# One piece of an MLP product moved from the first attention steps back into the MLP, with the second key tile's scores put ahead of it

## The chip, the core and the metric

The kernel runs on one NeuronCore of a Trainium2 chip. Five engines work side by side, each with its own queue of instructions that it takes in order: TensorE (PE; its loads of weights are listed as PEld), VectorE (DVE), ScalarE (ACT), GpSimd (POOL) and SyncE (SP, which here only issues transfers). An instruction whose inputs are not ready stops its engine, and all that is queued behind it, until they are. Matrix products land in PSUM, which has eight banks of 128 x 512 float32 values. The metric is the device time of one execution in microseconds (us), lower is better.

## The reference

For x of shape 2048 x 448 (one sequence) two branches are computed and mixed token by token:

```python
g = _sigmoid((x * gate_w).sum(-1, keepdims=True))
# A: attention, 16 heads of 28, one shared key and value head
q = (x @ wq) as 16 heads;  k = x @ wk;  v = x @ wv
o = softmax(q k^T * 28 ** -0.5) v
a = o @ wo
# B: token mixing by shifted columns, then an MLP
h  = _gelu(_layernorm(x) @ w1)
x1 = x + shifted(h) @ w2
b  = x1 + _gelu(_layernorm(x1) @ w3) @ w4      # w3: 448 x 1792, w4: 1792 x 448
out = g * a + (1 - g) * b
```

The change touches the last 128 of the 1792 rows of w4, for the last 512 tokens only, and the first three of the sixteen key tiles of the first attention unit.

## The kernel before

The program has three stages, written in the order in which each engine is to run its instructions: the schedule is manual, so an engine's queue is the order of the Python statements.

**First stage (0 to about 125 us).** Queries, keys, values and the gate; the token mixing branch; x1. The queries are written to DRAM (`qd`) and read back later, 512 tokens of four heads at a time, by `q_load` (four transfers on SP's queue).

**MLP (about 125 to 399 us).** For each of four blocks b of 512 tokens, `w3_part(b, f)` makes one 128 x 512 piece f (0 to 13) of the hidden layer: eleven products in fp32r, one of the float32 formats, with each operand split into a high and a low part. ScalarE applies the gelu twice, to an fp32r tile `gh` and a float32 tile `gf`, and VectorE forms the low part `gl = gf - gh`. Two pieces later `w4_part(f, t, ...)` adds the piece's product with w4 into four PSUM accumulators `acc[t]`, one for 128 tokens each: three matmuls (`gh`·`w4h`, `gh`·`w4l`, `gl`·`w4h`) for each t, so twelve matmuls a piece. After the last piece VectorE adds `acc[t]` to `x1`. The weights come in seven pairs of pieces, each loaded by SP and split by `split_w3` and `split_w4` during block 0.

In the kernel before, piece 13 of block 3 is an exception. Its gelu is kept as one float32 tile `gf_late`, its part of w4 was loaded as a plain float32 tile `w4_late`, and its product is left for the attention stage: eight *jobs* (`w4_products` and `w4_add`), one for each 128 tokens and each half of the 448 columns. A job is four float32 matmuls side by side in the array (`by_columns`, line 844; the profile counts two instructions for each) and one VectorE instruction (line 879) that weighs the result by 1 - g and adds it to x1.

**Attention (about 396 us to the end).** There are 16 units u (four token blocks times four groups of four heads) and 16 key tiles of 128 keys in each. For one unit and key tile, `scores` makes four heads' scores, 128 keys x 512 queries each, in three rounds of four matmuls that run side by side in four row groups of the array (line 204). `exps` (line 257, ScalarE) turns them into the tile `p`. `values` (line 893) multiplies p by the values.

A *step* c of the main loop handles two key tiles, 2c and 2c + 1; there are 128 steps. The eight PSUM banks are four *singles* and two *pairs* of two adjacent banks. The even tile of a step has heads 0 and 1 in two singles and heads 2 and 3 in one pair; VectorE copies the pair to the tile p in SBUF (line 954) and ScalarE exponentiates it there later, which frees the pair early. The odd tile uses the other two singles and the other pair, which ScalarE reads directly. After the scores of a step stand the values of the step before (32 instructions, written into the singles that the exps have emptied), and after those at most one job. In ScalarE's queue a step is: two singles, two singles, one pair, and last the exp of the copied tile (`p<-p`). So one `p<-p` row marks one step.

Steps 0 and 1 fill this pipeline. Tile 0 is computed at the end of the MLP, between the w4 products of piece 11 and of piece 12. In step 0 of the kernel before come tile 1 (four singles), tile 2 (both pairs, which are the four accumulators' banks: `pair_0` lies over acc 0 and 3, `pair_1` over acc 1 and 2) and three jobs. Step 1 makes tile 3 and the values of tiles 0 and 1. Steps 3, 5, 7, 9 and 11 hold one job each (`IDLE`), and the jobs of `wo` begin in step 12, one a step.

**Queues around the change.** At the start of the attention stage SP issues one 896 KB transfer of `wof` (the weights wo, first used in step 12) and behind it the four transfers of `q_fetch(1)`, the queries of unit 1, into `qr`. The memory that `wof` gets is that of `gh` tiles of the MLP, so this transfer waits for the last matmul that reads the last of them. In VectorE's queue `q_begin(1)` stands at step 2: a cast of `qr` to the fp32r tile `qh_1` (line 193), ahead of the copy of step 2's pair. In TensorE's queue, in the middle of step 2's values, stand sixteen small matmuls (`max_part`, line 211) that read `qh_1` and write into that same pair.

Of the kernel before, what the change touches and what calls it, by code (L numbers as in the profile page):

```python
# [17 lines left out]
P = 128  # L18
S = 2048
D = 448  # L20
H = 16
DH = 28
F = 1792
C = D // 4
NB = S // 512
NT = S // P
NF = F // P
# [15 lines left out]
def gated_mix_kernel(  # L43
# [64 lines left out]

    def split_w_high(raw, wh, wl):
        nc.scalar.copy(wh[:, 0:3, :], raw[:, 0:3, :])  # L110
        nc.gpsimd.memset(f32(wh)[64:128, 3, :], 0.0)
        nc.scalar.copy(wh[0:64, 3, :], raw[0:64, 3, :])
        nc.scalar.copy(wl[64:128, 3, :], raw[64:128, 3, :])

# [4 lines left out]

    def split_w(raw, wh, wl):  # L120
        split_w_high(raw, wh, wl)
        split_w_low(raw, wh, wl)
# [133 lines left out]
    def exps(p, heads, source=None):  # L256
        nc.scalar.activation(p[:, heads], p[:, heads] if source is None else source, AF.Exp, scale=SCALE)  # L257
# [4 lines left out]
    with tc.tile_pool(name="s1b", bufs=1) as s1b, \  # L262
# [329 lines left out]
        ql0 = late.tile([P, 512], F32R, name="ql0")  # L592
        gf_late = late.tile([P, 512], F32, name="gf_late")
        w4_late = late.tile([P, D], F32, name="w4_late")
        bigs = ctx.enter_context(tc.tile_pool(name="bigs", bufs=1, side="right", reuse_waits="tile"))
# [5 lines left out]
        def big(name):  # L601
            return bigs.tile([P, 2048], F32, tag="big", bufs=2, name=name)
# [12 lines left out]
        def split_w3(i):  # L615
            split_w(raw3[i], w3h[i], w3l[i])

# [49 lines left out]
    with tc.tile_pool(name="s2", bufs=1, reuse_waits="tile") as s2, \  # L667
# [11 lines left out]
        def w3_part(b, f):  # L679
            i, k = divmod(f, 2)  # L680
            ps = mm_tile(f"g_{b}_{f}")
            proj(ps, w3h[i][:, :, k * P:(k + 1) * P], w3l[i][:, :, k * P:(k + 1) * P], *acts[b])
            if (b, f) == (NB - 1, NF - 1):
                nc.scalar.activation(gf_late, ps, AF.Gelu_apprx_tanh)
                return None
            gh = s2.tile([P, 512], F32R, tag="gh", bufs=3, name=f"gh_{b}_{f}")
            gl = s2.tile([P, 512], F32R, tag="gl", bufs=3, name=f"gl_{b}_{f}")
            gf = s2.tile([P, 512], F32, tag="gf", bufs=1, name=f"gf_{b}_{f}")
            nc.scalar.activation(gh, ps, AF.Gelu_apprx_tanh)  # L689
            nc.scalar.activation(gf, ps, AF.Gelu_apprx_tanh)  # L690
            nc.vector.tensor_sub(gl, gf, f32(gh))  # L691
            return gh, gl

        def w4_part(f, t, g, acc, stop=NF - 1):
# [4 lines left out]
            nc.tensor.matmul(ps, gh[:, tok], w4h[i][:, k, :], start=(f == 0), stop=False)  # L699
            nc.tensor.matmul(ps, gh[:, tok], w4l[i][:, k, :], start=False, stop=False)  # L700
            nc.tensor.matmul(ps, gl[:, tok], w4h[i][:, k, :], start=False, stop=(f == stop))  # L701

        for b in range(NB):
            acc = [ps2.tile([P, 512], F32, tag="acc", bufs=4, name=f"acc_{b}_{t}") for t in range(4)]
            gs = {}
            for f in range(NF):
# [43 lines left out]
            if b == NB - 1:  # L750
                singles = [mm_tile("bank_0"), mm_tile("bank_1"), misc_tile("bank_2"), max_tile("bank_3")]
                scores(0, 0, singles)
                nc.scalar.activation(first, powt, AF.Exp)
                p_first = big("p_0_0").rearrange("p (j n) -> p j n", j=4)
                for j in range(4):
                    exps(p_first, slice(j, j + 1), singles[j].unsqueeze(1))
            for t in range(4):
                w4_part(NF - 2, t, gs[NF - 2], acc, NF - 2 if b == NB - 1 else NF - 1)
                if b + 1 < NB:
                    ln_split(b + 1, t, t + 1)  # L760
            for t in range(4):
                if b < NB - 1:
                    w4_part(NF - 1, t, gs[NF - 1], acc)
                xt = x1[:, 4 * b + t, :]
                nc.vector.tensor_add(xt, xt, acc[t][:, 0:D])
# [4 lines left out]
    with tc.tile_pool(name="s3", bufs=1, reuse_waits="tile") as s3, \  # L770
# [70 lines left out]
        def by_columns(ps, a, t, w, start=True, stop=True):  # L841
            for i in range(4):
                c = t * P + 32 * i
                nc.tensor.matmul(ps[32 * i:32 * i + 32, :], a[:, c:c + 32], w, start=start, stop=stop,  # L844
                                 tile_position=(0, 32 * i))
# [27 lines left out]

        def w4_products(t, ps, cols):
            by_columns(ps, gf_late, t, w4_late[:, cols])

        def w4_add(t, ps, cols):
            n = NT - 4 + t
            nc.vector.scalar_tensor_tensor(x1[:, n, cols], ps, gi[:, n:n + 1], x1[:, n, cols],
                                           op0=ALU.mult, op1=ALU.add)  # L880

        p_of = {0: p_first}

# [13 lines left out]

        jobs = [(w4_products, w4_add, (t,), cols) for t in range(4) for cols in halves]
        left, right, both, front = slice(0, 1), slice(1, 2), slice(2, 4), slice(0, 2)
        sums, norms, later = [], [], []  # L900
# [16 lines left out]
        def run_jobs(ps, n):  # L917
            job_adds(job_products(ps, n))

        NC = NU * NT // 2  # L920
        JOBS_0 = (2, 1)
        IDLE = range(2, 12, 2)
        HINTS = {8 * NT // 2 + 4: [mybir.EngineType.SP],
                 14 * NT // 2 - 2: [mybir.EngineType.DVE, mybir.EngineType.Activation]}
        for c in range(NC):
# [3 lines left out]
            if c == 0:  # L929
                pb = score_tiles(u, 1, s2, s3_, s0, s1)  # L930
                for j, ps in enumerate((s2, s3_, s0, s1)):
                    exps(pb, slice(j, j + 1), ps.unsqueeze(1))
                pa = score_tiles(u, 2, *(q[:, h] for q in pairs for h in range(2)))
                nc.vector.tensor_copy(pa[:, front], pairs[0])
# [210 lines left out]
```

## Time and profile before

| | us |
|---|---|
| runs, three | 911.51, 911.80, 913.12 |
| median | 911.80 |
| profiled execution | 911.48 |
| its span (first to last instruction) | 909.70 |
| ScalarE busy in 500 to 600 us | 99.64 of 100 |
| TensorE busy in 500 to 600 us | 100.00 of 100 |
| loads of weights (PEld) busy in 500 to 600 us | 56.55 of 100 |

Times in the rows of the trace are counted from the start of the span. A row of the timeline gives the start, the busy time, engine, line, operation, output and input tile, shape and count of instructions; in square brackets stands how long the engine had been idle before it and what ended that. Matmuls are pipelined, so the busy times of neighbours overlap, and the distance between two starts is what one costs. The same holds for ScalarE: exps that follow each other start 0.48 us apart though each is listed with 0.6 us.

### The profile page before, as it was taken

How to read it: one execution, taken by the hardware profiler on the slowest of the kernel's cores; microseconds unless marked ns; L12 is line 12 of the kernel's file. 1: busy time of each engine (PE TensorE's matmuls, PEld its weight loads, DVE VectorE, ACT ScalarE, POOL GpSimd, SP SyncE). 2: the span in 40 equal slices, each digit the busy share in tenths (PEclk: the TensorE clock that was granted, in tenths of full speed). 3: DMA queues.
4: the chain of work that ended last, by engine and by line, in shares of the span. 5: the costliest groups of instructions: out<-in, count | busy, mean ns of one | idle time of the engine just before them, and what ended most of it. 6: DMA issues, size and time to landing. Idle time of an engine off the chain costs nothing.

```text
span 909.7 us, 24149 instructions
## 1 busy us (share of the span) xinstructions
PE 903.1 (99%) x10360; PEld 626.8 (69%) x10360; DVE 515.8 (57%) x960; ACT 632.6 (70%) x1003; POOL 79.1 (9%) x116
## 2 busy tenths in 40 slices
PE   9999999999999999999999999999999999999998
PEld 6788888888888888875555555555555555555554
DVE  3665273631441531136766777676767667767665
ACT  5542444332132231269999999999999999999995
POOL 3243320200000520020000000000000000000000
PEclk9999999999999999999999999999999999999999
DMA  8832653120110120010000001000011000010001
GB/s 294 289 103 61 147 167 129 37 70 1 39 49 2 22 65 1 1 52 24 14 25 14 24 15 56 23 25 17 25 33 36 24 14 25 15 55 14 15 14 44
DMA packets 40726, 47.31 MB, mean 52 GB/s; under 512 B 10152, under 2 KB 28904, under 8 KB 40616
## 3 DMA queue, kind: packets, MB, share of 16 engines
q1 hardware_dynamic: 37448, 40.43, 15.2%
q10 hardware_dynamic: 3168, 5.31, 1.6%
q8 instruction: 82, 1.34, 0.6%
q14 instruction: 28, 0.23, 0.1%
HBM read 32.56 MB, written 11.67 MB: 49 GB/s over the span
## 4 chain that ended last, share of the span: by engine, by line
PE 97%; ACT 2%; DMA 1%; DVE 0%; issue 0%; SPq 0%
PE bank L893 26%; PE bank L204 20%; PE bank L844 6%; PE acc L701 5%; PE acc L699 5%; PE acc L700 5%; PE g L135 4%; PE g L137 4%; PE g L136 4%; PE pair L204 2%; ACT p L257 2%; PE hs L475 1%; PE hs L476 1%; PE g L138 1%; PE g L139 1%; PE h L136 1%
## 5 line engine op out<-in xcount | busy, mean ns | idle before, releaser
L257 ACT ACTIVATE p<-bank 128x512 f32<-128x512 f32 x514 | 265.9, 605 | 4.4 <-POOL pick L866 1.5
L893 PE MATMUL bank<-p,vext 128*32 128x256 f32 x4064 | 247.7, 382 | 1.0 <-ACT p L257 1.0
L893 PEld LDWEIGHTS bank<-p,vext 128*32 128x32 f32 x4064 | 117.9, 110 | 115.9 <-ACT p L257 53.0
L954 DVE COPY p<-pair 128x1024 f32<-128x1024 f32 x125 | 153.0, 1224 | 57.9 <-PE pair L204 40.9
L689 ACT ACTIVATE gh<-g 128x512 fp32r<-128x512 f32 x55 | 32.9, 598 | 181.7 <-PE g L139 181.7
L818 DVE TENSOR_TENSOR o<-o,bank 128x256 f32<-128x256 f32 x222 | 93.5, 421 | 80.4 <-PE bank L893 72.3
L257 ACT ACTIVATE p<-p 128x1024 f32<-128x1024 f32 x126 | 138.0, 1096 | 0.0
L257 ACT ACTIVATE p<-pair 128x1024 f32<-128x1024 f32 x129 | 136.8, 1060 | 0.0
L691 DVE TENSOR_TENSOR gl<-gf,gh 128x512 fp32r<-128x512 f32 x55 | 38.6, 702 | 164.9 <-ACT gf L690 164.9
L204 PE MATMUL bank<-qh,kh 32*128 32x512 f32 x514 | 114.8, 443 | 0.0
L204 PE MATMUL pair<-qh,kh 32*128 32x512 f32 x510 | 114.0, 443 | 0.0
L204 PE MATMUL bank<-qh,kl 32*128 32x512 f32 x514 | 101.8, 389 | 0.0
L204 PE MATMUL bank<-ql,kh 32*128 32x512 f32 x514 | 101.6, 390 | 0.0
L204 PE MATMUL pair<-qh,kl 32*128 32x512 f32 x510 | 101.3, 389 | 0.0
L204 PE MATMUL pair<-ql,kh 32*128 32x512 f32 x510 | 100.9, 389 | 0.0
L204 PEld LDWEIGHTS bank<-qh,kh 32*128 32x128 f32 x514 | 48.0, 182 | 61.3 <-issue 38.7
L701 PE MATMUL acc<-w4h,gl 128*128 128x448 f32 x220 | 80.7, 367 | 0.0
L699 PE MATMUL acc<-w4h,gh 128*128 128x448 f32 x220 | 80.2, 364 | 0.0
L700 PE MATMUL acc<-w4l,gh 128*128 128x448 f32 x220 | 79.8, 363 | 0.0
L844 PE MATMUL bank<-wof,on 128*32 128x224 f32 (+1 forms) x984 | 69.6, 357 | 0.0
L135 PE MATMUL g<-ah,w3h 128*128 128x512 f32 x168 | 65.4, 389 | 0.0
L136 PE MATMUL g<-al,w3h 128*128 128x512 f32 x168 | 65.4, 389 | 0.0
(206 smaller groups left out, 1394.1 us busy)
## 6 DMA issues: line engine op xcount, KB each, us to landing
qd<-qf ACTq DMA_DIRECT2D x15, 256.0 KB
rb<-rd SPq DMA_DIRECT2D x15, 256.0 KB
x<-in_x_dram SPq DMA_DIRECT2D x4, 896.0 KB
xd<-xt SPq DMA_DIRECT2D x16, 224.0 KB
w34raw<-in_w_dram SPq DMA_DIRECT2D x7, 512.0 KB
qr<-qd SPq DMA_DIRECT2D x64, 56.0 KB
w34raw<-in_w_dram SPq DMA_DIRECT2D x7, 448.0 KB
out_dram<-ot SPq DMA_DIRECT2D x14, 224.0 KB
```

The source lines that it names most:

```text
L135: nc.tensor.matmul(ps, wh[:, c, :], ah[:, c, :], start=(c == 0), stop=False)
L136: nc.tensor.matmul(ps, wh[:, c, :], al[:, c, :], start=False, stop=False)
L204: nc.tensor.matmul(ps[j], k[h, keys], q[h, :], start=(r == 0), stop=(r == 2), tile_position=(32 * j, 0))
L257: nc.scalar.activation(p[:, heads], p[:, heads] if source is None else source, AF.Exp, scale=SCALE)
L691: nc.vector.tensor_sub(gl, gf, f32(gh))
L699: nc.tensor.matmul(ps, gh[:, tok], w4h[i][:, k, :], start=(f == 0), stop=False)
L700: nc.tensor.matmul(ps, gh[:, tok], w4l[i][:, k, :], start=False, stop=False)
L701: nc.tensor.matmul(ps, gl[:, tok], w4h[i][:, k, :], start=False, stop=(f == stop))
L818: nc.vector.tensor_add(o, o, pv)
L844: nc.tensor.matmul(ps[32 * i:32 * i + 32, :], a[:, c:c + 32], w, start=start, stop=stop, tile_position=(0, 32 * i))
L893: nc.tensor.matmul(pv[32 * j:32 * j + 32, :], vext[:, kt, :], p_of[k][:, j, qs], start=(k == ks[0]), stop=(k == ks[-1]), tile_position=(0, ...
L954: nc.vector.tensor_copy(pa[:, both], pairs[0])
```

## The change

Piece 13 of block 3 is treated like every other piece: its gelu gives `gh`, `gf` and `gl`, and `w4_part` adds its product into the accumulators, in the order of t 1, 2, 0, 3 (in all four blocks). `gf_late`, `w4_late`, its load, and the eight jobs are gone. The scores and exps of key tile 1 stand ahead of these twelve matmuls, in the four singles, and write a tile of another pool. Step 0 keeps only tile 2: two heads in the two singles that step 1 doesn't use, two in `pair_1`, which VectorE copies and ScalarE exponentiates from SBUF. A loop without jobs remains for steps 2 to 11, and `IDLE` goes. In `split_w3` the copy of the doubled last rows of w3 moves from ScalarE to GpSimd.

```diff
-    def split_w_high(raw, wh, wl):
+    def split_w_high(raw, wh, wl, last=nc.scalar.copy):
...
-        nc.scalar.copy(wl[64:128, 3, :], raw[64:128, 3, :])
+        last(wl[64:128, 3, :], raw[64:128, 3, :])
...
         def split_w3(i):
-            split_w(raw3[i], w3h[i], w3l[i])
+            split_w(raw3[i], w3h[i], w3l[i], nc.gpsimd.tensor_copy)
...
-            if (b, f) == (NB - 1, NF - 1):
-                nc.scalar.activation(gf_late, ps, AF.Gelu_apprx_tanh)
-                return None
...
+        def first_exps(kt, singles):
+            p = big(f"p_0_{kt}").rearrange("p (j n) -> p j n", j=4)
+            for j in range(4):
+                exps(p, slice(j, j + 1), singles[j].unsqueeze(1))
+            return p
...
-                nc.sync.dma_start(w4_late, w4[F - P:F, :])
...
-            for t in range(4):
-                if b < NB - 1:
-                    w4_part(NF - 1, t, gs[NF - 1], acc)
+            if b == NB - 1:
+                scores(0, 1, singles)
+                p_first.append(first_exps(1, singles))
+            for t in (1, 2, 0, 3):
+                w4_part(NF - 1, t, gs[NF - 1], acc)
                 xt = x1[:, 4 * b + t, :]
                 nc.vector.tensor_add(xt, xt, acc[t][:, 0:D])
...
-        jobs = [(w4_products, w4_add, (t,), cols) for t in range(4) for cols in halves]
+        jobs = []
...
             if c == 0:
-                pb = score_tiles(u, 1, s2, s3_, s0, s1)
-                for j, ps in enumerate((s2, s3_, s0, s1)):
-                    exps(pb, slice(j, j + 1), ps.unsqueeze(1))
-                pa = score_tiles(u, 2, *(q[:, h] for q in pairs for h in range(2)))
-                nc.vector.tensor_copy(pa[:, front], pairs[0])
-                for ps, n in zip((s2, s3_), JOBS_0):
-                    run_jobs(ps, n)
-                exps(pa, both, pairs[1])
-                exps(pa, front)
                 pairs.reverse()
+                pa = score_tiles(u, 2, s2, s3_, pairs[0][:, 0], pairs[0][:, 1])
+                exps(pa, left, s2.unsqueeze(1))
+                exps(pa, right, s3_.unsqueeze(1))
+                nc.vector.tensor_copy(pa[:, both], pairs[0])
+                exps(pa, both)
                 continue
...
-            adds = job_products(s0[:, q1], 0 if c in IDLE or c == 1 else 1)
+            adds = job_products(s0[:, q1], 1)
```

What this does to the queues, at the two places where the most moves. TensorE, from the last round of scores of key tile 1 on, in the kernel before (`bank_0` to `bank_3` are the singles; the numbers behind a name count buffers):

```order
L204 MATMUL bank_0_3208<-qh0_1048,kl_75 128x512
L204 MATMUL bank_1_3209<-qh0_1048,kl_75 128x512
L204 MATMUL pair_0_3257<-qh0_1048,kh_1047 128x512 x2
L204 MATMUL pair_1_3258<-qh0_1048,kh_1047 128x512 x2
L204 MATMUL pair_0_3257<-ql0_1049,kh_1047 128x512 x2
L204 MATMUL pair_1_3258<-ql0_1049,kh_1047 128x512 x2
L204 MATMUL pair_0_3257<-qh0_1048,kl_75 128x512 x2
L204 MATMUL pair_1_3258<-qh0_1048,kl_75 128x512 x2
L844 MATMUL bank_2_3210<-w4_late_1051,gf_late_1050 32x224 x8
L844 MATMUL bank_3_3211<-w4_late_1051,gf_late_1050 32x224 x4
L204 MATMUL bank_0_3208<-qh0_1048,kh_1047 128x512
L204 MATMUL bank_1_3209<-qh0_1048,kh_1047 128x512
```

The same place in the changed kernel, from the end of the same round on; of the twelve matmuls of piece 13 only the first three and the scores behind the last three are shown in two pieces:

```order
L204 MATMUL bank_2_3213<-qh0_1048,kl_75 128x512
L204 MATMUL bank_3_3214<-qh0_1048,kl_75 128x512
L701 MATMUL acc_3_1_2800<-w4h_6_1515,gh_3_13_3193 128x448
L702 MATMUL acc_3_1_2800<-w4l_6_1516,gh_3_13_3193 128x448
L703 MATMUL acc_3_1_2800<-w4h_6_1515,gl_3_13_3194 128x448
```

And the end of piece 13 in TensorE's queue of the changed kernel:

```order
L702 MATMUL acc_3_3_2802<-w4l_6_1516,gh_3_13_3193 128x448
L703 MATMUL acc_3_3_2802<-w4h_6_1515,gl_3_13_3194 128x448
L204 MATMUL bank_2_3213<-qh0_1048,kh_1047 128x512
L204 MATMUL bank_3_3214<-qh0_1048,kh_1047 128x512
L204 MATMUL pair_1_3290<-qh0_1048,kh_1047 128x512 x2
```

Twelve fp32r matmuls now stand between the scores of tile 1 and those of tile 2, and the three jobs behind tile 2 (twelve float32 matmuls) are gone.

VectorE's queue of the kernel before, from the last addition to x1 to the maximum of step 2 (`qr` is where the queries of unit 1 land):

```order
L765 TENSOR_TENSOR x1_70<-x1_70,acc_3_3_2804 128x448
L934 COPY p_0_2_3308<-pair_0_3257 128x1024
L879 SCALAR_TENSOR_TENSOR x1_70<-bank_2_3210,gi_78,x1_70 128x224 x2
L879 SCALAR_TENSOR_TENSOR x1_70<-bank_3_3211,gi_78,x1_70 128x224
L814 COPY o_0_3351<-bank_2_3210 128x256
L814 COPY o_0_3351<-bank_3_3211 128x256
L193 CAST qh_1_3377<-qr_3259 128x512
L954 COPY p_0_4_3374<-pair_1_3258 128x1024
L818 TENSOR_TENSOR o_0_3351<-o_0_3351,bank_0_3208 128x256
L218 TENSOR_REDUCE mr_1_3423<-pair_1_3258 128x4x4
```

The same place in VectorE's queue of the changed kernel:

```order
L766 TENSOR_TENSOR x1_70<-x1_70,acc_3_3_2802 128x448
L925 COPY p_0_2_3323<-pair_1_3290 128x1024
L815 COPY o_0_3352<-bank_2_3213 128x256
L815 COPY o_0_3352<-bank_3_3214 128x256
L193 CAST qh_1_3378<-qr_3291 128x512
L941 COPY p_0_4_3375<-pair_1_3290 128x1024
L819 TENSOR_TENSOR o_0_3352<-o_0_3352,bank_0_3211 128x256
L218 TENSOR_REDUCE mr_1_3424<-pair_1_3290 128x4x4
```

The additions of jobs are gone; the cast of `qr` stays ahead of the copy of tile 4's pair. SP's queue keeps its order too, `wof` and then the four transfers into `qr`; but the last reader of the memory under `wof` was piece 12's last matmul on `gh_3_12`, and is now the last matmul of piece 13 that reads `gh_3_13`, the row of line 702 above.

More of the change, by code (lines that the diff above doesn't have):

```diff
@@ L118, in split_w_low, with split_w @@
         nc.vector.tensor_tensor(wl[0:64, 3, :], raw[0:64, 3, :], f32(wh)[0:64, 3, :], ALU.subtract)
-    def split_w(raw, wh, wl):
-        split_w_high(raw, wh, wl)
+    def split_w(raw, wh, wl, last):
+        split_w_high(raw, wh, wl, last)
         split_w_low(raw, wh, wl)
@@ L592, in gated_mix_kernel @@
         ql0 = late.tile([P, 512], F32R, name="ql0")
-        gf_late = late.tile([P, 512], F32, name="gf_late")
-        w4_late = late.tile([P, D], F32, name="w4_late")
+        late.tile([P, 512 + D], F32, name="gap_late")
         bigs = ctx.enter_context(tc.tile_pool(name="bigs", bufs=1, side="right", reuse_waits="tile"))
@@ L692, in w3_part, with w4_part @@
             return gh, gl
-        def w4_part(f, t, g, acc, stop=NF - 1):
+        def first_exps(kt, singles):
[3 more added lines that the diff above has]
+            return p
+        def w4_part(f, t, g, acc):
             i, k = divmod(f, 2)
@@ L700, in w4_part @@
             nc.tensor.matmul(ps, gh[:, tok], w4l[i][:, k, :], start=False, stop=False)
-            nc.tensor.matmul(ps, gl[:, tok], w4h[i][:, k, :], start=False, stop=(f == stop))
+            nc.tensor.matmul(ps, gl[:, tok], w4h[i][:, k, :], start=False, stop=(f == NF - 1))
         for b in range(NB):
@@ L753, in gated_mix_kernel @@
                 nc.scalar.activation(first, powt, AF.Exp)
-                p_first = big("p_0_0").rearrange("p (j n) -> p j n", j=4)
-                for j in range(4):
-                    exps(p_first, slice(j, j + 1), singles[j].unsqueeze(1))
+                p_first = [first_exps(0, singles)]
             for t in range(4):
-                w4_part(NF - 2, t, gs[NF - 2], acc, NF - 2 if b == NB - 1 else NF - 1)
+                w4_part(NF - 2, t, gs[NF - 2], acc)
                 if b + 1 < NB:
                     ln_split(b + 1, t, t + 1)
-            for t in range(4):
-                if b < NB - 1:
-                    w4_part(NF - 1, t, gs[NF - 1], acc)
+            if b == NB - 1:
[3 more added lines that the diff above has]
+                w4_part(NF - 1, t, gs[NF - 1], acc)
                 xt = x1[:, 4 * b + t, :]
@@ L872, in gated_mix_kernel @@
         weigh_x1(NT - 4, NT)
[L874 to L882, printed above, removed]
+        p_of = dict(enumerate(p_first))
         def score_tiles(u, kt, first, second, third, fourth):
@@ L896, in values @@
                     p_of.pop(k)
-        jobs = [(w4_products, w4_add, (t,), cols) for t in range(4) for cols in halves]
-        left, right, both, front = slice(0, 1), slice(1, 2), slice(2, 4), slice(0, 2)
+        jobs = []
+        left, right, both = slice(0, 1), slice(1, 2), slice(2, 4)
         sums, norms, later = [], [], []
@@ L920, in gated_mix_kernel @@
         NC = NU * NT // 2
-        JOBS_0 = (2, 1)
-        IDLE = range(2, 12, 2)
         HINTS = {8 * NT // 2 + 4: [mybir.EngineType.SP],
```

## The prediction

> **What bounds the kernel now.** I read the page first, then the busy times by stretch, then the timelines of single engines around the seam between MLP and attention. The page:
>
> ```profile
> PE 903.1 (99%) x10360; PEld 626.8 (69%) x10360; DVE 515.8 (57%) x960; ACT 632.6 (70%) x1003; POOL 79.1 (9%) x116
> PE 97%; ACT 2%; DMA 1%; DVE 0%; issue 0%; SPq 0%
> ```
>
> The first line is each engine's busy time and share of the span, the second the chain of work that ended last: nearly all TensorE. By stretch (columns PE, PEld, DVE, ACT, POOL):
>
> ```profile
> 120.00:140.00 20.00, 20.00 (x93) 17.48 (x94) 12.37 (x25) 10.68 (x20) 0.82 (x3) 1.00 0.61 197
> ...
> 340.00:400.00 60.00, 60.00 (x299) 52.04 (x297) 9.93 (x15) 15.53 (x29) 0.47 (x2) 1.00 0.00 1
> ...
> 500.00:600.00 100.00, 100.00 (x1708) 56.55 (x1704) 71.14 (x136) 99.64 (x155) 0.00 (x0) 1.00 0.09 30
> ```
>
> In the MLP TensorE is the only full engine, so a matmul added there is paid whole. In the attention TensorE and ScalarE are both full. Which of them sets a step is seen in ScalarE's queue, where one `p<-p` row closes each step:
>
> ```profile
> 413.07 1.10 ACT L257 ACTIVATE p<-p 128x1024 f32<-128x1024 f32 x1
> ...
> 417.03 1.09 ACT L257 ACTIVATE p<-p 128x1024 f32<-128x1024 f32 x1
> 417.98 2.11 ACT L257 ACTIVATE p<-bank 128x512 f32<-128x512 f32 x4
> ...
> 420.78 1.15 ACT L257 ACTIVATE p<-p 128x1024 f32<-128x1024 f32 x1
> ...
> 424.73 1.09 ACT L257 ACTIVATE p<-p 128x1024 f32<-128x1024 f32 x1
> ...
> 447.83 1.09 ACT L257 ACTIVATE p<-p 128x1024 f32<-128x1024 f32 x1
> ...
> 451.73 1.10 ACT L257 ACTIVATE p<-p 128x1024 f32<-128x1024 f32 x1
> ```
>
> These are steps 3, 4, 5, 6, 12 and 13. From 3 to 4 it is 3.96, from 4 to 5 3.75, from 5 to 6 3.95. Step 3 holds a job and step 4 none. Inside the short step the exps follow without a hole (417.03 to 417.98 is 0.95 for the wide exp), so 3.76 is ScalarE's own time, and a job in the step before makes TensorE late by about 0.19. With a job in every step it is 3.90 (12 to 13).
>
> **The direct price of the piece.** TensorE at the seam:
>
> ```profile
> 395.88 0.51 PE L204 MATMUL bank<-qh,kh 32*128 32x512 f32 x4
> ...
> 396.78 0.47 PE L699 MATMUL acc<-w4h,gh 128*128 128x448 f32 x1
> ...
> 399.11 0.36 PE L701 MATMUL acc<-w4h,gl 128*128 128x448 f32 x1
> 399.40 0.51 PE L204 MATMUL bank<-qh,kh 32*128 32x512 f32 x4
> ...
> 400.20 0.49 PE L204 MATMUL pair<-qh,kh 32*128 32x512 f32 x4
> ...
> 401.09 1.34 PE L844 MATMUL bank<-w_late,gf_late 128*32 128x224 f32 x24
> 402.37 0.50 PE L204 MATMUL bank<-qh,kh 32*128 32x512 f32 x1
> ```
>
> The twelve matmuls of piece 12 take 396.78 to 399.40, which is 2.62. Scores ahead of such matmuls take 0.90 (395.88 to 396.78). ScalarE at the same place:
>
> ```profile
> 396.87 2.07 ACT L257 ACTIVATE p<-bank 128x512 f32<-128x512 f32 x4 [1.21 <-PE bank L204]
> 400.44 2.07 ACT L257 ACTIVATE p<-bank 128x512 f32<-128x512 f32 x4 [1.50 <-POOL pick L866]
> 402.37 1.06 ACT L257 ACTIVATE p<-pair 128x1024 f32<-128x1024 f32 x1
> 403.27 1.09 ACT L257 ACTIVATE p<-p 128x1024 f32<-128x1024 f32 x1
> 404.22 1.12 ACT L257 ACTIVATE p<-bank 128x512 f32<-128x512 f32 x2
> ```
>
> Before, ScalarE waits 1.50 once, between tiles 0 and 1, and from 400.44 on it never stands still for long. Now a second hole opens. Up to tile 1's scores (399.40) nothing changes in time, and tile 1's exps end as before, free for the next at 402.37. But piece 13 stands from 399.40 + 0.90 = 400.30 to 402.92, and only then come tile 2's scores. Scores to first exp took 1.04 (399.40 to 400.44), so tile 2 starts at 403.96 in place of 402.37: 1.59 lost.
>
> Tile 2 also changes form: two single exps, then VectorE's copy of the pair, then a wide exp from SBUF. VectorE:
>
> ```profile
> 397.69 2.44 DVE L765 TENSOR_TENSOR x<-x,acc 128x448 f32<-128x448 f32 x4 [7.25 <-PE acc L701]
> 401.19 1.22 DVE L934 COPY p<-pair 128x1024 f32<-128x1024 f32 x1 [1.06 <-PE pair L204]
> ...
> 406.17 0.49 DVE L193 CAST qh<-qr 128x512 fp32r<-128x512 f32 x1 [0.27 <-DMA qr<-qd]
> 406.57 1.20 DVE L954 COPY p<-pair 128x1024 f32<-128x1024 f32 x1
> ...
> 408.74 0.42 DVE L218 TENSOR_REDUCE mr<-pair 128x16 f32<-128x256 f32 x1
> ```
>
> The copy starts with the scores' end, 0.99 after their start (400.20 to 401.19), so at 403.91, and ends at 405.13. The wide exp starts there and takes 0.95, so tile 3 starts at 406.08 in place of 404.22: in all 1.86 late. I take 1.9 for everything behind it. The four additions to x1 move with the piece (last one ends at 400.13 + 3.52 = 403.65); tile 3's pair needs it, and tile 3's scores come at 403.7 by the same distances, so this costs 0 to 0.1.
>
> **A transfer that becomes late.** SP's queue, and TensorE's in step 2:
>
> ```profile
> 399.50 0.40 SPq L773 DMA_DIRECT2D wof<-in_wo_dram  x1
> 400.09 2.56 SPq L189 DMA_DIRECT2D qr<-qd  x4
> ```
>
> ```profile
> 407.20 1.07 PE L893 MATMUL bank<-p,vext 128*32 128x256 f32 x16
> 408.09 0.30 PE L211 MATMUL pair<-khd,qh 128*32 128x64 bf16 x16
> ...
> 409.19 0.50 PE L204 MATMUL bank<-qh,kh 32*128 32x512 f32 x2
> ```
>
> `wof` was issued at 399.50, just after piece 12's last matmul (399.11 + 0.36). It now waits for piece 13's last use of `gh`, one matmul (2.62 / 12, some 0.2) before the end of the piece, which comes 0.90 + 2.62 = 3.52 later: a shift of 3.3. The four `qr` transfers stand behind it in SP's queue, and before the change they already landed last: the cast at 406.17 had waited 0.27 for them. With the same distance the cast comes at 409.5, the copy behind it at 409.9, and that ends at 411.1. The sixteen small matmuls (line 211) write into the pair that this copy reads; without the transfer they would come at 408.09 + 1.9 = 410.0. So TensorE waits 1.15 there, with half of step 2's values and all of step 3 behind it. ScalarE's `p<-p` of step 2 needs the copy too, but only at about 411.05, so that costs 0.1 at most and inside the same wait. Step 3 starts 1.9 + 1.15 = 3.05 late. The trace has no row for `qr` with `wof` issued this late. From below the wait is 0 (a landing more than 1.2 sooner), from above 1.9 (a landing 0.7 later, more than twice the 0.27). I take 1.15, from the row that shows this very landing as the last to arrive.
>
> **The gain.** From step 3 to step 12 there are nine steps, 413.07 to 447.83, 34.76. Without the jobs of steps 3, 5, 7, 9 and 11 each should take ScalarE's 3.76, that is 33.81: 0.95 gained. Step 12's first `wo` job then follows a step without one, as step 5's did: 3.95 in place of 3.90, 0.05 given back. The three jobs of step 0 (401.09 to 402.37, 1.28 of TensorE) gain nothing: ScalarE was working off tile 1 meanwhile.
>
> **What I cost at nothing.** A second gelu and VectorE's low part for piece 13:
>
> ```profile
> 389.12 0.59 ACT L690 ACTIVATE gf<-g 128x512 f32<-128x512 f32 x1
> ...
> 393.55 0.60 ACT L684 ACTIVATE gf_late<-g 128x512 f32<-128x512 f32 x1 [3.83 <-PE g L139]
> ```
>
> The gelu is 0.5 more on ScalarE and moves what stands behind it (the load of the exp table) back by as much; the 1.21 idle ahead of the exps at 396.87 covers it. If it didn't, all would slip by up to 0.5. The low part has until 400.7 on an idle VectorE (7.25 ahead of 397.69). Seven copies of 64 x 256 go from ScalarE to GpSimd:
>
> ```profile
> L113 ACT CAST w3l<-w34raw x7: 403/405/406, 116.7 to 168.9; 64x256 fp32r<-64x256 f32 x7
> ```
>
> ```profile
> 115.85 1.08 POOL L357 CAST kh<-kl 128x512 fp32r<-128x512 f32 x1
> ...
> 118.80 0.81 POOL L111 MEMSET w3h<- 64x256 f32 x3
> 124.88 0.82 POOL L111 MEMSET w3h<- 64x256 f32 x3 [5.27 <-PE hs L478]
> ```
>
> A GpSimd copy twice as wide cost up to 1.08, so each of these is below that. The first is done by 120.2, and GpSimd was idle for 5.27 before 124.88, ahead of the MLP's first products. TensorE is never short of weights in the MLP before (20.00 of 20 busy from 120 to 140, where the splits run), so ScalarE's seven times 0.41 bring nothing. If a copy were late, its whole lateness would show on TensorE. The missing load of `w4_late` and the missing additions of jobs were on idle queues.
>
> **Sum.** 1.9 + 1.15 - 0.95 + 0.05 = +2.15 on the profiled execution's 911.48, so 913.6. The median of the runs is 0.32 higher, 911.80, so a median of 914.0; I give 913.8, between the two. What a measurement of this kernel can tell from no change is about 0.2%, 1.8 us: the forecast lies just beyond it.
>
> **Rivals.** (a) *The transfer arrives in time.* If `qr` lands by 408.2, step 2 isn't held up: 1.9 - 0.95 + 0.05 = +1.0, so 912.8, not slower by what can be told. For it: the transfers' own issue takes only 2.56, and nothing else is on the queue. Against it: before, with the same queue, VectorE waited for them. It decides from a landing 1.2 sooner than the shift of 3.3 gives. (b) *ScalarE alone bounds the attention, and the jobs were free.* Then 1.9 + 1.15 = +3.05, so 914.9. For it: 99.64 of 100 busy. Against it: steps behind a job are 0.19 longer, in five pairs alike. [...] (c) *TensorE alone bounds all.* Then what counts is 2.62 added against eight jobs of 1.28 / 3 removed, 3.41: -0.8, so 911.0. For it: the chain at 97%. Against it: the hole of 1.50 in ScalarE's row of 400.44, which shows that exps not fed in time are lost for good.
>
> **Chances.** Forecast 0.68, (a) 0.17, (b) 0.06, (c) 0.05, something I don't see, 0.04, likely dearer. The range 912.1 to 915.2 holds the forecast with both ends of the late transfer's wait (-1.15, +0.75), (a) and (b). Of the forecast's 0.68 I put 0.48 beyond +1.8 and 0.20 within; with (b) and most of the unseen that makes slower 0.57; (a), a part of (c) and the 0.20 make same 0.39; faster 0.04.
>
> **What would show it.** Right: a hole of about 1.6 in ScalarE's row ahead of tile 2; the cast of `qr` near 409.5 with over 2 of idle that a DMA ends; the small matmuls of step 2 waiting about 1.1 for that copy; nine steps of 3.76 from step 3 to 12. Wrong: a cast that doesn't wait, steps still of 3.9, or TensorE waiting for GpSimd's copies between 125 and 170.

## The result and the profile after

The changed kernel takes 914.01 us (median of 14 runs, 913.50 to 914.82), the kernel before, beside it, 911.75 (14 runs, 911.39 to 913.12). The ratio is 1.0024, with a 95% interval of 1.0017 to 1.0030: slower by 2.3 us, a quarter of a per cent; a ratio of 1 lies outside the interval. The forecast was 913.8. The first page lines after, busy times and chain:

```profile
PE 904.1 (99%) x10308; PEld 627.2 (69%) x10308; DVE 513.2 (56%) x953; ACT 629.3 (69%) x998; POOL 82.7 (9%) x123
PE 94%; ACT 3%; DMA 1%; DVE 1%; issue 0%; SPq 0%; DVEq 0%
```

TensorE has 52 matmuls fewer (64 of the eight jobs gone, 12 of the piece added) and is still 99% busy; the chain now goes 3% through ScalarE for 2%. These lines say little. ScalarE's timeline at the seam (start, duration, what ran, idle before it and what ended that):

```profile
397.80 2.06 ACT L257 ACTIVATE p<-bank 128x512 f32<-128x512 f32 x4 [0.77 <-issue]
401.33 2.07 ACT L257 ACTIVATE p<-bank 128x512 f32<-128x512 f32 x4 [1.47 <-PE bank L204]
404.80 1.09 ACT L257 ACTIVATE p<-bank 128x512 f32<-128x512 f32 x2 [1.40 <-PE pair L204]
406.13 1.06 ACT L257 ACTIVATE p<-p 128x1024 f32<-128x1024 f32 x1 [0.25 <-DVE p L925]
407.09 1.07 ACT L257 ACTIVATE p<-bank 128x512 f32<-128x512 f32 x2
409.00 2.06 ACT L257 ACTIVATE p<-bank 128x512 f32<-128x512 f32 x4
...
411.83 1.09 ACT L257 ACTIVATE p<-p 128x1024 f32<-128x1024 f32 x1
413.81 2.06 ACT L257 ACTIVATE p<-bank 128x512 f32<-128x512 f32 x4 [0.89 <-PE pair L204]
```

These rows are the first exps of tiles 0, 1 and 2, tile 2's wide exp, tile 3, step 2, step 2's wide exp, and step 3. The first row already stands 0.93 later than its 396.87 of before, ahead of anything that the change does to the seam, while the same MLP code puts it at 396.77 to 397.44 in the other profiled executions below, so I read it as scatter between executions. In what follows, distances are counted from this row. Then tile 2 comes 1.50 later than before (7.00 for 5.50), with the new hole of 1.40 ahead of it; tile 3 is 1.94 later (9.29 for 7.35); step 3's first exps find another 0.89 of idle.

TensorE, VectorE and SP's queue, changed kernel:

```profile
400.27 0.51 PE L204 MATMUL bank<-qh,kh 32*128 32x512 f32 x4
401.18 0.47 PE L701 MATMUL acc<-w4h,gh 128*128 128x448 f32 x1
...
403.51 0.37 PE L703 MATMUL acc<-w4h,gl 128*128 128x448 f32 x1
403.81 0.50 PE L204 MATMUL bank<-qh,kh 32*128 32x512 f32 x2
...
411.71 0.30 PE L211 MATMUL pair<-khd,qh 128*32 128x64 bf16 x16 [0.62 <-DVE p L941]
```

```profile
410.10 0.43 DVE L193 CAST qh<-qr 128x512 fp32r<-128x512 f32 x1 [2.12 <-DMA qr<-qd]
410.44 1.22 DVE L941 COPY p<-pair 128x1024 f32<-128x1024 f32 x1
```

```profile
403.70 0.40 SPq L774 DMA_DIRECT2D wof<-in_wo_dram  x1
404.14 1.77 SPq L189 DMA_DIRECT2D qr<-qd  x4
```

Piece 13 stands from 401.18 to 403.81, 2.63, where it was put. `wof` is issued 3.27 later than before, the four `qr` transfers behind it; VectorE's cast waits 2.12 for them, the copy of step 2's pair stands behind the cast, and TensorE's sixteen small matmuls wait 0.62 for the copy.

The wide exps that close steps 3, 4, 9, 10, 11, 12 and 13, changed kernel:

```profile
416.63 1.09 ACT L257 ACTIVATE p<-p 128x1024 f32<-128x1024 f32 x1
...
420.39 1.15 ACT L257 ACTIVATE p<-p 128x1024 f32<-128x1024 f32 x1
...
439.20 1.40 ACT L257 ACTIVATE p<-p 128x1024 f32<-128x1024 f32 x1
...
443.02 1.39 ACT L257 ACTIVATE p<-p 128x1024 f32<-128x1024 f32 x1
...
446.95 1.28 ACT L257 ACTIVATE p<-p 128x1024 f32<-128x1024 f32 x1
...
450.70 1.33 ACT L257 ACTIVATE p<-p 128x1024 f32<-128x1024 f32 x1
...
454.85 1.10 ACT L257 ACTIVATE p<-p 128x1024 f32<-128x1024 f32 x1
```

The steps are 3.75 to 3.78 now, as forecast, except from 9 to 10 (3.82) and 10 to 11 (3.93), where the maxima of the next group are worked out; from 3 to 12 it is 34.07 for 34.76. From 12 to 13, the first step with a `wo` job, it is 4.15 for 3.90.

### The profile page after: what moved, and what is told of

The parts are those of the page before. It is cut to its first block, busy times and chain, and to the rows that moved or that the text cites. A ratio compares the mean times of both kernels' runs of the same rounds, so it can differ in the third digit from the quotient of the medians.

```text
span 913.0 us, 24055 instructions
## 1 busy us (share of the span) xinstructions
PE 904.1 (99%) x10308; PEld 627.2 (69%) x10308; DVE 513.2 (56%) x953; ACT 629.3 (69%) x998; POOL 82.7 (9%) x123
## 4 chain that ended last, share of the span: by engine, by line
PE 94%; ACT 3%; DMA 1%; DVE 1%; issue 0%; SPq 0%; DVEq 0%
PE bank L886 25%; PE bank L204 19%; PE bank L845 5%; PE acc L703 5%; PE acc L701 5%; PE acc L702 5%; PE g L136 4%; PE g L137 4%; PE g L135 4%; ACT p L257 3%; PE pair L204 2%; PE hs L475 1%; PE hs L476 1%; PE g L138 1%; PE g L139 1%; PE h L136 1%
## 5 line engine op out<-in xcount | busy, mean ns | idle before, releaser
L257 ACT ACTIVATE p<-bank 128x512 f32<-128x512 f32 x516 | 268.6, 618 | 6.3 <-PE pair L204 2.6
```

## The experiments

The table gives, for each kernel, how much later than before its wide exp of a step starts (both counted from tile 0's first exp), and in the last column but one how much longer the time from the last wide exp to the end of the span is (16.25 before). All are worked out from the rows of the profiled executions. Of the kernel before, the prediction shows tile 0's first exp (396.87) and steps 3, 12 and 13; step 2 and the last wide exp are

```profile
409.15 1.09 ACT L257 ACTIVATE p<-p 128x1024 f32<-128x1024 f32 x1
...
893.42 1.09 ACT L257 ACTIVATE p<-p 128x1024 f32<-128x1024 f32 x1
```

The last column is the median of the runs, less that of the kernel before beside it.

| kernel | step 2 | step 3 | step 12 | step 13 | last | end | median |
|---|---|---|---|---|---|---|---|
| the change | +1.75 | +2.63 | +1.95 | +2.20 | +2.34 | +0.05 | +2.26 |
| queries' transfers first | +1.75 | +1.84 | +1.16 | +1.40 | +1.75 | +0.02 | +1.69 |
| cast behind the copy | +1.76 | +1.84 | +1.15 | +1.39 | +1.74 | -0.01 | +1.67 |
| no piece | +1.37 | +1.44 | +0.75 | +1.00 | +1.11 | +0.07 | +1.13 |
| half the piece | +1.36 | +1.44 | +0.75 | +0.99 | +1.02 | +0.12 | +1.19 |
| no piece, tile 2 in the pairs | +0.30 | +0.14 | -0.49 | -0.26 | +0.01 | +0.08 | +0.62 |
| before, no jobs | 0.00 | +0.04 | -0.65 | -0.40 | -0.31 | +1.68 | +1.45 |
| the same, mark moved | 0.00 | 0.00 | -0.68 | -0.45 | -0.10 | +1.81 | +1.55 |
| the same, copies on GpSimd | -0.11 | -0.09 | -0.78 | -0.54 | -0.24 | -0.01 | -0.38 |
| the change, copies on ScalarE | +1.80 | +2.40 | +1.71 | +1.95 | +2.07 | +1.59 | +3.80 |
| the change, six copies more | +1.75 | +2.54 | +1.85 | +2.09 | +2.40 | +1.65 | +3.89 |
| before, tile 1 early | +1.22 | +1.05 | +1.11 | +1.11 | +1.71 | -0.01 | +1.44 |

**Is it the transfer?** The changed kernel with the queries' transfers issued ahead of `wof`:

```diff
-        nc.sync.dma_start(wof, wo.rearrange("(g p) n -> p g n", p=P))
...
         q_fetch(1)
+        nc.sync.dma_start(wof, wo.rearrange("(g p) n -> p g n", p=P))
```

> The changed kernel with the four transfers of unit 1's queries issued ahead of the wo weights' transfer; nothing else moves. Theory (the late transfer holds VectorE's cast, the copy behind it and with that TensorE's small matmuls of step 2): the cast no longer waits for a transfer, the small matmuls no longer wait for the copy, and the 0.8 us that step 2 lost in the changed kernel's trace comes back: 914.0 - 0.8 = 913.2, a ratio to the kernel before of 1.0016. Rival (the wait is hidden, step 2 is late because of piece 13 alone): no change, 914.0. In the trace the distance from the exps of tile 2 to those of step 3's first tile (404.80 to 413.81, 9.01, in the changed kernel) falls to about 8.2 by the theory and stays 9.0 by the rival.

And with the transfers left late, but VectorE's cast behind the copy:

```diff
-            if i == 2 and u == 0:
-                q_begin(1)
...
             if 1 < c < NC - 1:
                 nc.vector.tensor_copy(pa[:, both], pairs[0])
...
+            if i == 2 and u == 0:
+                q_begin(1)
```

> The changed kernel with VectorE's cast of unit 1's queries put behind the copy of step 2's pair; the transfers stay late. Theory (the cast's place ahead of the copy is what turns a late transfer into a stall): the copy and with it ScalarE's last exp of step 2 go on time, the small matmuls wait only for the cast, which is done at about 410.5 on the changed kernel's clock, before they are due at 410.9, so the gain is the same 0.8 us: 913.2, ratio 1.0016. Rival (the transfer itself holds the small matmuls, since they read the cast queries): part of the wait stays, 913.6 to 914.0.

The first took 913.34 us (ratio to before 1.0019, 1.0010 to 1.0028), the second 913.32 (1.0018, 1.0009 to 1.0028): each 0.7 below the change, or 0.6 when each is set against the kernel before beside it. Transfers first, VectorE's timeline:

```profile
407.54 0.58 DVE L193 CAST qh<-qr 128x512 fp32r<-128x512 f32 x1
408.90 1.22 DVE L941 COPY p<-pair 128x1024 f32<-128x1024 f32 x1 [0.78 <-PE pair L204]
```

Cast behind, VectorE's and TensorE's:

```profile
408.42 1.23 DVE L939 COPY p<-pair 128x1024 f32<-128x1024 f32 x1 [1.27 <-PE pair L204]
409.56 0.42 DVE L193 CAST qh<-qr 128x512 fp32r<-128x512 f32 x1
```

```profile
410.08 0.30 PE L211 MATMUL pair<-khd,qh 128*32 128x64 bf16 x16
```

In both, the copy waits for TensorE and no longer the other way round, and the small matmuls run without a wait, 13.12 behind tile 0's first exp (397.44 and 396.96 in these two) for 13.91 in the change. One mend takes away the transfer's lateness, the other only the order on VectorE, and both gain the same 0.79 at step 3: the price is the copy queued behind the waiting cast, and the chain of the prediction is shown link by link. Its size scatters: in two more kernels with the same seam (the last two of the change in the table) the small matmuls wait 0.32 and 0.52, and step 3 stands at +2.40 and +2.54, so the price is 0.56 to 0.79.

**Is it the piece?** The changed kernel without piece 13's twelve matmuls in the last block (that product is left out):

```diff
+                if b < NB - 1:
                     w4_part(NF - 1, t, gs[NF - 1], acc)
```

> The changed kernel without the twelve matmuls of piece 13 in block 3, so the last 128 rows of w4 are left out for the last 512 tokens; its gelu, the order of the rest and the additions to x1 stay. Theory (their 2.62 us open a hole on ScalarE ahead of tile 2 and push the wo weights' transfer and the queries behind it): the direct 1.9 us and the 0.8 us of the late transfer go, and what is left against the kernel before is the gain from the missing jobs: 914.0 - 2.7 = 911.3, ratio 0.9995. Rival, TensorE alone bounds: 914.0 - 2.6 and no more, about the same number, but then the cast of the queries would still wait 2 us for its transfer. Rival, the piece is hidden: 914.0.

912.78 us (1.0014, 1.0005 to 1.0024), not the 911.3 expected: only 1.2 below the change, and 0.6 to 0.8 of that is the transfer, which comes in time when piece 13 no longer reads `gh`. At step 2 the whole piece is worth 0.38 of 1.75. TensorE shows why:

```profile
399.25 0.51 PE L204 MATMUL bank<-qh,kh 32*128 32x512 f32 x4
401.93 0.98 PE L204 MATMUL bank<-qh,kh 32*128 32x512 f32 x2 [1.71 <-ACT p L257]
```

Tile 1's scores and then nothing for 1.71: tile 2's scores go into single banks that tile 1's exps are still reading. The piece fills a gap that the change itself has made. Half the piece (token tiles 1 and 2 alone; the other half of the product is left out) should then be free:

```diff
+                if b < NB - 1 or t in (1, 2):
                     w4_part(NF - 1, t, gs[NF - 1], acc)
```

> The changed kernel with piece 13 only for the token tiles 1 and 2 of the last block, six matmuls for twelve (the other half of that product is left out). Theory (two bounds lie beside each other, and without the piece TensorE waits 1.71 for a single bank that ScalarE frees): the first 1.7 of the piece's 2.6 are free, so half a piece, 1.3, costs nothing: TensorE still waits about 0.4 for ScalarE ahead of tile 2's scores, the transfer is 1.3 later and still in time, 912.8 like the run without the piece. Rival (each matmul of the piece is paid whole): halfway between 912.8 and 914.0, 913.4.

912.73 us (1.0012, 1.0003 to 1.0022), the same as without it. TensorE, half the piece:

```profile
401.37 0.37 PE L703 MATMUL acc<-w4h,gl 128*128 128x448 f32 x1
402.03 0.98 PE L204 MATMUL bank<-qh,kh 32*128 32x512 f32 x2 [0.29 <-ACT p L257]
```

It still waits for the bank, 0.29 after the six matmuls. And without the piece, but with tile 2 in the two pairs, as before (the product is left out):

```diff
-                pa = score_tiles(u, 2, s2, s3_, pairs[0][:, 0], pairs[0][:, 1])
+                pa = score_tiles(u, 2, *(q[:, h] for q in pairs for h in range(2)))
```

> The changed kernel without piece 13's twelve matmuls in the last token block (that product is left out, so the output lacks it) and with tile 2's scores in the two pairs, as before the change. Theory (what is left of the change's price without its piece is the single banks: tile 2's scores wait there for tile 1's exps): the hole ahead of tile 2 is gone, the wide exp runs into tile 3 as before, step 2 starts like before, and the missing jobs gain the 0.4 that all the traces show, so 911.3. Rival 1 (the hole in the run without the piece has another cause): 912.8 as that run. Rival 2 (missing jobs cost time in themselves, as the run of the kernel before without jobs seems to say): 913.1.

912.16 us (1.0008, 0.9999 to 1.0018), above the 911.3 expected, though by the rows it ends within 0.1 of before; its ten runs spread from 911.18 to 913.83, and a ratio of 1 lies inside the interval. The hole ahead of tile 2 is gone, as expected; ScalarE's row of tile 2:

```profile
402.67 1.06 ACT L257 ACTIVATE p<-pair 128x1024 f32<-128x1024 f32 x1
```

It follows tile 1's exps (400.74) without a wait. So the new form of tile 2, its banks and the order of exps that goes with them, costs about 1.1 at step 2 (1.37 less 0.30), the piece 0.4 on top. Not expected were 0.30 lost at step 2 and 0.3 at a later step (below). At step 2 TensorE waits 0.26 for VectorE's last addition to x1, which frees the pair; the copy of the pair then starts 0.40 later than before, and TensorE waits 0.83 for it ahead of tile 3's pair. That the three jobs of step 0 are missing is not the reason: the kernel before without its jobs, below, has step 2 at +0.00.

**What are the jobs worth?** The kernel before with an empty list of jobs (the product of the last piece of `w4` is left out):

```diff
-        jobs = [(w4_products, w4_add, (t,), cols) for t in range(4) for cols in halves]
+        jobs = []
```

> The kernel before without its eight jobs, so the last 128 rows of w4 are left out for the last 512 tokens and nothing takes their place. This prices the gain alone. As predicted (a job delays the step behind it by 0.19, five of them, 0.05 given back): 911.75 - 0.9 = 910.85, ratio 0.9990. As the changed kernel's trace reads (steps 3 to 12 gained 0.69 and step 12 to 13 gave 0.25 back): 911.75 - 0.44 = 911.3, ratio 0.9995. ScalarE alone bounds: 911.75. TensorE alone bounds: eight jobs of 0.43, 908.3. In the trace the steps from 3 to 12 are 3.76 where no job stands, with one or two longer ones around steps 9 to 11, and the step from 12 to 13 is about 4.14.

913.10 us (1.0015, 1.0006 to 1.0024): slower, where every theory had said faster or the same. The table says where: the steps gain 0.31 in all, and the end is 1.68 longer. In the end the kernel loads a flag and branches over the code that would redo the work. The span with ScalarE's last row, and the packets of the instruction queue from that branch to the end, before without jobs:

```profile
core 0 of [0], span 911.0 us
...
905.02 0.16 ACT L1059 ACTIVATE redo<-pair 1x1 int32<-1x1 f32 x1 [7.05 <-PE pair L1057]
```

```profile
q14 instruction: 4, 0.03, 2.9%
```

and of the kernel before:

```profile
core 0 of [0], span 909.7 us
...
905.43 0.16 ACT L1059 ACTIVATE redo<-pair 1x1 int32<-1x1 f32 x1 [7.05 <-PE pair L1057]
```

```profile
q14 instruction: 3, 0.02, 2.6%
```

From this row to the end it is 6.0 for 4.3. In the trace's records, in which branches stand too, ScalarE's next instruction comes 2.93 behind the branch, for 0.48 before and in the change; the instruction queue moves four packets for three. ScalarE has five records more ahead of the branch here, all of them waits for semaphores: without the jobs its instructions are the same, but they wait more often. I first took the mark that announces this branch for the cause, and moved ScalarE's eight steps later, again without jobs:

```diff
-                 14 * NT // 2 - 2: [mybir.EngineType.DVE, mybir.EngineType.Activation]}
+                 14 * NT // 2 - 2: [mybir.EngineType.DVE],
+                 15 * NT // 2 - 2: [mybir.EngineType.Activation]}
```

> The kernel before without its eight jobs (the product of the last piece of w4 is left out), with ScalarE's mark for the branch at the end eight steps later. Theory (the run without jobs lost its time behind ScalarE's last branch, 2.93 to the next instruction for 0.48, which is code that wasn't there): the end is as short as before, the steps are 0.4 shorter, 911.3. Rival (the loss does not hang on the mark): 913.1 as without it.

913.09 us (1.0015, 1.0006 to 1.0025), 3.06 behind the branch: that theory fell, and that code was missing there is a guess which no trace shows. The next run was meant for the copies that the prediction costs at nothing, the change with them back on ScalarE:

```diff
-            split_w(raw3[i], w3h[i], w3l[i], nc.gpsimd.tensor_copy)
+            split_w(raw3[i], w3h[i], w3l[i], nc.scalar.copy)
```

> The changed kernel with the last copy of each of the seven splits back on ScalarE. Prediction (these copies cost nothing on either engine): 914.0, as the changed kernel. Rival (the GpSimd copies hold TensorE up, or ScalarE's time was worth something): 0.3 or more to either side.

915.34 us (1.0039, 1.0025 to 1.0053), on the rival's side but for neither of its reasons: it is 1.5 further above before than the change, none of it in the steps (+2.07 at the last one, for +2.34) and all of it at the end: 2.74 behind the branch. In the seven kernels run so far with 0.48, the branch is ScalarE's record 1209 or 1210, in the three with a late one 1215 or 1216. So the number of instructions ahead of it was the next suspect: the change with six tiny copies more on ScalarE, in the second block of the MLP, which nothing reads:

```diff
+                if b == 1 and f == 3:
+                    for _ in range(6):
+                        nc.scalar.copy(first, powt)
```

> The changed kernel with six ScalarE copies of 128x4 more, in the second token block of the MLP, where ScalarE is idle most of the time; nothing reads what they write. Theory (in the three runs whose last branch stood as ScalarE's record 1215 or 1216 from the start, the next instruction came 2.74 to 3.06 behind it, in the seven with 1209 or 1210 0.48; it is the number of instructions ahead of the branch that decides): the branch stands at 1216, the end of the kernel is 1.5 to 1.7 longer, 915.6. Rival (copies on an idle ScalarE cost nothing, and the late end had another cause): 914.0.

915.68 us (1.0043, 1.0030 to 1.0057), as foretold. The end of this kernel:

```profile
core 0 of [0], span 913.9 us
...
907.98 0.16 ACT L1049 ACTIVATE redo<-pair 1x1 int32<-1x1 f32 x1 [7.04 <-PE pair L1047]
```

and of the changed kernel:

```profile
core 0 of [0], span 913.0 us
...
908.69 0.16 ACT L1046 ACTIVATE redo<-pair 1x1 int32<-1x1 f32 x1 [7.04 <-PE pair L1044]
```

From the row to the end it is 5.9 for 4.3. Six instructions on an idle engine, 700 us ahead of the branch, cost 1.6. With that, the jobs could be measured: before without jobs (the product is left out), and with the seven copies on GpSimd as in the change, so seven ScalarE instructions fewer.

> The kernel before without its eight jobs (the product of the last piece of w4 is left out), with the last copy of the seven w3 splits on GpSimd, as the change has it: seven ScalarE instructions fewer ahead of the branch. Theory: the end is as short as before (0.48 behind the branch), so the run shows what the jobs alone are worth; by the step rows that all traces share, 0.69 gained up to step 12 and 0.25 given back there, and up to 0.3 for one hold-up of TensorE further on, so 911.1 to 911.5. Rival (jobs taken away cost time): 913.1 as without the copies moved.

911.41 us (0.9997, 0.9988 to 1.0006), with 0.48 behind the branch again. The jobs are worth 0.38 by the medians, 0.25 by the rows; a ratio of 1 lies inside the interval, so it is the rows and not the runs' times that show a gain.

**Would a version in between be faster?** The kernel before with tile 1's scores ahead of piece 12's last token tile (the product is whole), with the queries' transfers first and the copies on GpSimd:

```diff
             for t in range(4):
+                if (b, t) == (NB - 1, 3):
+                    scores(0, 1, singles)
...
+                        exps(p_second, slice(j, j + 1), singles[j].unsqueeze(1))
                 w4_part(NF - 2, t, gs[NF - 2], acc, NF - 2 if b == NB - 1 else NF - 1)
```

> The kernel before with tile 1's scores and exps ahead of the last three matmuls of piece 12, the four query transfers ahead of wo's, and the GpSimd copies of the change (whole result). Theory (the hole of 1.50 in ScalarE's row ahead of tile 1 is lost for good, and the scores can come 0.65 earlier): tile 1's exps 0.65 earlier and with them all that follows, as far as TensorE keeps up, so 911.0 (910.8 to 911.4). Rival (TensorE's own work ahead of step 2 decides): 911.6, no change.

913.23 us (1.0015, 1.0006 to 1.0024), slower by 1.4: both theories missed. TensorE and ScalarE:

```profile
400.88 0.37 PE L701 MATMUL acc<-w4h,gl 128*128 128x448 f32 x1
401.97 0.50 PE L204 MATMUL pair<-qh,kh 32*128 32x512 f32 x4 [0.71 <-DVE x L770]
```

```profile
400.31 2.07 ACT L257 ACTIVATE p<-bank 128x512 f32<-128x512 f32 x4 [0.90 <-PE bank L204]
403.02 1.02 ACT L257 ACTIVATE p<-pair 128x1024 f32<-128x1024 f32 x1 [0.64 <-PE pair L204]
```

Tile 1 does come 0.61 earlier. But tile 1's scores used to stand between piece 12 and tile 2's scores, and covered VectorE's last addition, which frees the pair. Now TensorE waits 0.71 for it, and the hole stands one tile later: tile 2's scores start 4.62 behind tile 0's first exp for 3.33 before, and ScalarE stands idle for another 0.84 ahead of step 2. No version with the whole result that was run beats the kernel before.

## Why the prediction was right, point by point

- **The sum.** +2.15 was forecast and +2.26 measured, +2.39 by the rows (+2.34 up to the last wide exp and 0.05 at the end). The late transfer and the shorter steps were the mechanisms forecast, with other sizes; the hole ahead of tile 2 has a second cause that the prediction didn't see. By the rows the sum is 1.75 for the seam, 0.79 for the transfer and 0.09 more up to step 3, then 0.69 gained, 0.25 given back, and 0.14 and 0.05 that were not forecast. The errors of the terms have both signs and nearly cancel: that the total came so close is luck.
- **The direct price, 1.9.** Tile 2 was forecast 1.59 later and tile 3 1.86; 1.50 and 1.94 came, 1.75 at step 2. The size stands, but its reading does not: the prediction charged all of it to the piece. It took "free for the next at 402.37" of ScalarE, and didn't ask when the banks are free. Without the piece 1.37 is left, and the first half of the piece is free. The two bounds, bank and piece, lie beside each other. So "a matmul added there is paid whole" fails for this piece.
- **The late transfer, 1.15: mis-sized.** `wof` moved by 3.27 (forecast 3.3), the cast waited 2.12 ("over 2"), the small matmuls came where forecast without the transfer (13.12 behind tile 0's first exp, forecast 13.13). But the four transfers were issued within 1.77, for 2.56 before, the cast started 0.33 sooner than forecast, and the term is 0.79 by the rows of two mends, 0.56 to 0.79 with the other executions of this seam, and 0.6 to 0.7 by the medians.
- **The gain, -0.95: mis-sized.** "Each should take ScalarE's 3.76" held for steps 3 to 8 and from 11 to 12. From 9 to 11 it is 7.75; before it was 7.70, with a job:

```profile
436.19 1.15 ACT L257 ACTIVATE p<-p 128x1024 f32<-128x1024 f32 x1
...
443.89 1.15 ACT L257 ACTIVATE p<-p 128x1024 f32<-128x1024 f32 x1
```

  There stand the sixteen small matmuls for the next group's maxima; that they make TensorE late with or without a job is read from their place and was not tested. All kernels without these jobs gain 0.63 to 0.69 from step 3 to 12, in place of 0.95.
- **Given back, 0.05: mis-sized.** The first `wo` job behind a long run without jobs costs 0.39 over a step without (4.15 for 3.76), not 0.19; 0.23 to 0.25 is given back. The missing jobs were worth 0.43 from step 3 to step 13, half of the 0.90 forecast.
- **Costed at nothing.** The second gelu: tile 0's exps come 1.05 after its scores' start, for 0.99 before; that holds. The three jobs of step 0 gained nothing, as forecast: without them TensorE waits 0.91 there for a bank that ScalarE frees, and step 2 starts at +0.00. The GpSimd copies held up nobody: they take 0.39 to 0.82 each, and TensorE's matmuls show no wait from 120 to 180. But "ScalarE's seven times 0.41 bring nothing" was wrong: left on ScalarE, they cost 1.5, by their number and not by their time (six tiny copies elsewhere bring 1.6 as well). The whole change with these copies on ScalarE took 915.34, above the forecast's range, so that they move with it is a second piece of luck.
- **Not seen.** Between step 13 and the last wide exp another 0.14 is lost on balance. One place behind step 59 costs 0.3 by itself, with 0.28 of idle on ScalarE:

```profile
634.56 1.09 ACT L257 ACTIVATE p<-p 128x1024 f32<-128x1024 f32 x1
635.93 2.06 ACT L257 ACTIVATE p<-bank 128x512 f32<-128x512 f32 x4 [0.28 <-PE bank L204]
```

  TensorE's records show one gap of 0.48 between two starts there, with no wait listed. The kernel before has none there; with the queries' transfers first it stands some 50 steps later. What causes it stays open.
- **The rivals.** (a), the transfer in time: it was not, though two small edits make it so (913.3). (b), the jobs free: 3.76 for 3.95 in the steps shows that they aren't, but the 0.43 up to step 13 lies halfway between the 0.90 forecast and nothing. (c), TensorE alone: the holes of 1.40 and 0.89 speak against it.

## What to carry to other kernels

Where work fills a stall, ask what else ends that stall: taking the work away shows whether the next bound (here a bank still being read, 1.71 of wait without the piece) lies just beneath. A load that an engine casts in order holds up all that is queued behind the cast (here the cast waited 2.12, and behind the copy it gained 0.79 at step 3); put the cast behind the work that others wait for. And before an experiment's time is put down to its edit, compare the ends of the two traces: the number of instructions ahead of a branch can cost more than the edit (here six copies more cost 1.6, and the jobs were worth 0.38).

## What the runs showed of the hardware that I had not expected

- **What follows a branch can come late by the number of instructions ahead of it.** With ScalarE's last branch at record 1203 to 1210 (nine kernels) the next instruction comes 0.48 behind it, at 1215 or 1216 (four kernels) 2.74 to 3.06, and the kernel ends 1.6 to 1.8 later. Six idle-time copies bring this about and seven copies fewer take it away; moving the mark that announces the branch by eight steps does not take it away (3.06). In the four late kernels three packets of the instruction queue (`q14`) start with the branch or up to 0.7 behind it, in the nine others two. A packet takes 0.3 to 0.6, less than the wait, so what the engine waits for is not shown. At which number the turn lies between 1210 and 1215, and why there, was not tried.
- **A listed duration isn't the distance to the next instruction.** In the run of short steps the wide exp's duration grows from 1.09 to 1.40 (steps 3 to 9) while the step stays at 3.75 to 3.78 and the next exp starts 0.95 behind it (417.58 behind 416.63), later 0.99 (440.19 behind 439.20).

```profile
417.58 2.10 ACT L257 ACTIVATE p<-bank 128x512 f32<-128x512 f32 x4
...
440.19 2.37 ACT L257 ACTIVATE p<-bank 128x512 f32<-128x512 f32 x4
```
